# Three of an expert's four first matrices are prepared during the second products before it, in groups at the ends of row pairs; scratch results go to PSUM

## The chip, the cores and the metric

One core of a Trainium2 chip runs the whole program. The metric is the time of one execution in microseconds (us) of the device; the median of three runs of the kernel before is 1100.38 us, from 1098.74 to 1102.79. Engines are named as the profile names them: PE (TensorE, matrix products), PEld (its weight loads), DVE (VectorE), ACT (ScalarE), POOL (GpSimd), SP (the engine whose queue issues the transfers, "SPq" in the trace).

## The reference, cut to what matters

Three stages follow each other: attention with a learned bias, a first gated layer (MoE1), and a second layer with eight experts (MoE2). Only the third is touched.

```python
def _moe2_ref(x, w_gate, w1, w2):           # x 1152x512, w1 8x512x1024, w2 8x1024x512
    logits = x @ w_gate
    P = np.exp(logits - logits.max())
    for _ in range(8):
        P /= P.sum(1, keepdims=True) + 1e-09
        P /= P.sum(0, keepdims=True) + 1e-09
        P *= N / E
    out = np.zeros((N, D))
    for e in range(E):
        h = np.maximum(x @ w1[e], 0.0)
        out += P[:, e:e + 1] * (h @ w2[e])
    return out
```

## The kernel before, in words

Attention and MoE1 end at about 333 us; the rest is MoE2. Each float32 matrix is scaled by a power of two and split into a high and a low float16 part, and a product is made as high·high + high·low + low·high.

**First products.** `up(n)` makes a quarter of one expert's first product: n = 4e + q, expert e, quarter q. Each quarter consists of seven block products (a Strassen-like scheme that needs seven where eight would do), each of twelve matmuls (L1222), into PSUM banks `x`, `y`, `z`. Between them ACT copies banks out (`snap`, L1232), DVE joins them (`join`, L1236), and the result goes through a relu into float16 parts `hh` (ACT, L1240) and `hl` (DVE, L1245). The calls of `then(seg)` between the products, seg 0 to 6, take steps from the dictionary `extra`, which the main loop fills.

**Second products.** Expert 0 is done plainly, in two halves, `down_0(0)` after n = 2 and `down_0(1)` after n = 4: nine tiles of twelve matmuls each (`plain`, L1328) into a PSUM tile of tag "d", of which the pool `ps_d` has two; `add` (L1317 on ACT for the first half, L1319 on DVE otherwise) moves a tile to `acc`. The steps of the dictionary `todo` stand behind the tiles. For experts 1 to 7 `down(e)` takes eight of nine row tiles as four pairs i = 0 to 3, each with seven block products (L1404) and four main products (L1409) into banks px, py, pz. DVE first makes sums of blocks of the activations for the next pair (`sums`, L1397, eight instructions per pair) and adds each bank to `acc` (L1319). The ninth tile is plain, in two pieces, one ahead of the pairs and one behind them. The calls `more(i, k)`, k = 0 to 4, inside pair i take steps from `todo`.

**The work between.** All that prepares the next weights is written as steps that these dictionaries place:

- `prep(n, k)`: quarter n of w1. Step 0 scales it on ACT (L919) and issues the next load; 1 and 2 make sums of its blocks on DVE (L923 to L928, four instructions); 3 splits the plain blocks (ACT L931, POOL L932), 4 and 5 the sums (ACT L935, POOL L938).
- `p2(e, j)`: row block j of expert e's w2: ACT scales (L1016) and rounds it (L1017), POOL makes the low part `w2l` (L1018), and the next load is issued.
- `split_b(e)`: eight differences of w2 blocks on DVE (L1309).
- `pe(e, i)`: the largest absolute value of a quarter of w1 (i < 4, DVE, L754) or of a block of w2 (i ≥ 4, ACT, L102, which also writes a scratch result `junk`).
- `send(e, kind)`: DVE joins those maxima into `pj` (L788), SP writes them to DRAM (`peakse<-pj`) and reads all 128 back to every partition (`all<-peakse`). `power(e, kind)`: DVE reduces `all` (L751) and makes the power of two by which w1 (kind 1) or w2 (kind 2) is scaled.
- `gains(h)`: the factors for `add`.

The program order of each engine is the order of these calls; each engine and SP's queue run their own instructions in that order, and wait where an input or a buffer is not ready.

Of the kernel before, what the change touches and what calls it, by code (L numbers as in the profile page):

```python
# [9 lines left out]
F32 = mybir.dt.float32  # L10
# [3 lines left out]
F16 = mybir.dt.float16  # L14
# [9 lines left out]
DM = H * D  # L24
FF1 = 768
NE = 8
# [26 lines left out]
def make_body(stop=None):  # L53
    def body(tc, a):
        nc = tc.nc
        ctx = ExitStack()
        V, A, G, T = nc.vector, nc.scalar, nc.gpsimd, nc.tensor
# [18 lines left out]
        with ctx, tc.manual_schedule():  # L76
# [22 lines left out]
            mo, jk = [], []  # L99
# [641 lines left out]
            def peak_get(n):  # L741
                peak_send(n)
                if n in peaks_d:
                    src = peaks_d.pop(n)
                    w = src.shape[0]
                    peaks_s[n] = scl.tile([128, 256], F32, tag="all", name="all", bufs=2)[:, 0:w]
                    dma(peaks_s[n], src.unsqueeze(0).to_broadcast([128, w]))

            def peak_in(n, out):
# [68 lines left out]
            def peak_pow(m, items):  # L818

                if items:  # L820
                    for i, (h, kind) in enumerate(items):
                        o = scl.tile([128, 4], F32, tag=f"pw{kind}", name="pw", bufs=4)
# [6 lines left out]
            with ExitStack() as mctx:  # L829
# [79 lines left out]
                def prep_f(n):  # L909
# [4 lines left out]
                    hi = w1s.tile([128, 7, 2, 128], F16, tag="w1h", name="w1h")  # L914
                    lo = w1s.tile([128, 7, 2, 128], F16, tag="w1l", name="w1l")
                    w1s_t[n] = hi, lo

                    def scale():
# [82 lines left out]

                w2t, w2s = {}, []

                def prep_2(i):
# [78 lines left out]
            with ExitStack() as ectx:  # L1083
                h_p = ectx.enter_context(pool("h_p", bufs=2))
                w2s.append(ectx.enter_context(pool("w2t", bufs=2)))
                tp = ectx.enter_context(pool("tp"))
                jp.append(tp)
                sk = ectx.enter_context(pool("sk"))
                ps_d = ectx.enter_context(pool("ps_d", bufs=2, space=PSUM))
                banks = []  # L1090

                def use_banks(name):
# [243 lines left out]
                def run(fs):  # L1336
                    for f in fs:
                        f()
# [13 lines left out]
                def down_0(h):  # L1352
# [5 lines left out]
                                4: prep(3, 4, 5) + p2(0, 5), 5: p2(0, 6) + pe(1, 5), 6: p2(0, 7) + pe(1, 6),  # L1358
                                7: pe(1, 7), 8: power(1, 1) + prep(4, 0)}
                    else:  # L1360
                        todo = {0: prep(5, 0), 1: prep(5, 1), 2: prep(5, 2, 3), 3: power(1, 2) + p2(1, 0) + prep(5, 4, 5),
                                4: p2(1, 1, 2), 5: p2(1, 3), 6: p2(1, 4), 7: p2(1, 5), 8: p2(1, 6, 7)}
# [8 lines left out]
                w2_at = {1: [(2, 1), (2, 1), (2, 2), (2, 4), (3, 0), (3, 1), (3, 2), (3, 3)],  # L1371
                         2: [(1, 0), (1, 1), (1, 2), (1, 4), (2, 0), (2, 1), (2, 3), (2, 4)],
                         3: [(0, 0), (0, 2), (1, 0), (1, 2), (1, 4), (2, 1), (2, 3), (3, 0)]}

                def down(e):

# [35 lines left out]
                    todo = {}  # L1412
                    put = lambda i, k, fs: todo.setdefault((i, k), []).extend(fs)
                    if e < NE - 1:
                        put(0, 2, pe(e + 1, 3) + send(e + 1, 1))
                        put(2, 1, power(e + 1, 1) + prep(4 * e + 4, 0))
                        for i, k, ks in ((2, 2, (1,)), (2, 3, (2,)), (2, 4, (3, 4)), (3, 0, (5,))):
                            put(i, k, prep(4 * e + 4, *ks))
                        for i, k, ks in ((3, 1, (0,)), (3, 2, (1,)), (3, 3, (2, 3)), (3, 4, (4, 5))):
                            put(i, k, prep(4 * e + 5, *ks))  # L1420
                        if e < 3:
                            put(*((2, 0), (1, 0))[e - 1], power(e + 1, 2))
                        for j, at in enumerate(w2_at[min(e, 3)]):
                            put(*at, p2(e + 1, j))
                        if e > 1:
                            for j in range(4):
                                put(3, 1 + j, pe(e + 2, 4 + j))
                        put(3, 2, pe(e + 2, 0))
# [12 lines left out]
                    for i in range(4):  # L1441
# [24 lines left out]
                        prod(z2, A22, T4, False)  # L1466
                        prod(y, two(s[4]), B22, False)
                        run(nxt[4])
                        more(i, 2)
                        prod(x, two(s[3]), T3, False)  # L1470
# [20 lines left out]
                for n in range(4 * NE):  # L1491
                    e, q = divmod(n, 4)
                    extra = {}
                    put = lambda seg, fs: extra.setdefault(seg, []).extend(fs)
                    if n == 2:
                        put(1, prep(3, 0))
                    if n == 3:
# [9 lines left out]
                    if n == 1 or e and q in (1, 2):  # L1507
                        for seg, ks in ((0, (0,)), (1, (1, 2)), (2, (3,)), (3, (4, 5))):
                            put(seg, prep(n + 1, *ks))
                    if e and q == (1 if e == 1 else 0):  # L1510
                        b_s = split_b(e)
                    if e == 1:
                        for seg, k in {1: ((4, 0), (6, 1)), 2: ((5, 2), (6, 3), (6, 4)), 3: ((2, 5), (4, 6), (5, 7))}.get(q, ()):
                            put(seg, [b_s[k]])
                        if q in (1, 2):
                            put(5, pe(2, q - 1))
                        if q == 3:
                            for seg, i in ((0, 4), (1, 5), (2, 6), (4, 7)):
                                put(seg, pe(2, i))
                    elif e:  # L1520
                        for seg, k in {0: ((2, 0), (4, 1), (6, 2)), 1: ((6, 3),), 2: ((6, 4),), 3: ((2, 5), (4, 6), (5, 7))}[q]:
                            put(seg, [b_s[k]])
                        if q == 0:
                            put(5, pe(e + 1, 1))
                        if e == 2:
                            if q in (0, 3):
                                for j, seg in enumerate((0, 1, 2, 4)):
                                    put(seg, pe(3, 4 + j + 4 * (q > 0)))
                            if q == 3:
                                put(5, send(3, 2))  # L1530
                        elif q == 0:
                            for j, seg in enumerate((0, 1, 2, 4)):
                                put(seg, pe(e + 1, 8 + j))
                            put(6, send(e + 1, 2))
                        elif q == 3:
                            put(0, power(e + 1, 2))
                    if e and q == 3:
                        put(1, pe(e + 1, 2))
                    if e and q == (3 if e == 1 else 2):
                        put(3, [lambda: gains(e + 1)])  # L1540
                    up(n, extra)
                    if n in (2, 4):
                        down_0(n // 2 - 1)
# [63 lines left out]
```

## Time and profile before

| | |
|---|---|
| median of three runs | 1100.38 us (1098.74 to 1102.79) |
| the profiled execution, its own time | 1097.79 us |
| its span | 1096.0 us |
| PE busy | 1032.0 us, 94% |
| DVE busy | 862.4 us, 79% |
| ACT busy | 607.0 us, 55% |
| POOL busy | 326.9 us, 30% |

The span is what the trace covers of the profiled execution; its own time is 1.8 us longer. Busy shares are averages over stages that differ, so the stages are read one by one: a row of the windows view gives, for one stretch of the span, each engine's busy time and the clock granted to PE as a share of full speed. The view by time lists single instructions with their start and duration, and in brackets the idle time of the engine just before one and what ended it.

### The profile page before, as it was taken

The page shows a single profiled execution, that of the slowest core. Times are in us where ns is not written, and L with a number is a line of the kernel's source. Part 1 is how long each engine was busy: PE and PEld are TensorE (multiplying, and loading weights), DVE is VectorE, ACT ScalarE, POOL GpSimd, SP SyncE. Part 2 cuts the span into 40 slices and gives each one's busy share as a digit, 9 for nine tenths or more (in the row PEclk, how much of TensorE's full clock was granted, in tenths as well). Part 3 has the DMA queues.
Part 4 walks back from the last instruction along what each step waited for, and adds up shares of the span by engine and source line. Part 5 has one row for each costly group of instructions (what it writes and reads, how often), then busy time and mean ns, then how long its engine had stood idle before and what let it go on. Part 6 is the DMA issues. An engine that isn't in the chain of part 4 may idle for free. (4 is left out here: it accounts for less than half of the span.)

```text
span 1096.0 us, 21984 instructions
## 1 busy us (share of the span) xinstructions
PE 1032.0 (94%) x8842; PEld 805.8 (74%) x8842; DVE 862.4 (79%) x1706; ACT 607.0 (55%) x1116; POOL 326.9 (30%) x228
## 2 busy tenths in 40 slices
PE   8999999999999999898999998999899899989998
PEld 3267778999997565677777776877777687777787
DVE  8977775999588768887688789769778976976874
ACT  9989884444167675653662574366166436614710
POOL 6943532222141033302322422221242222124200
PEclk9999999999999999999999999999999999999999
DMA  6986652434210211202202210211121020100001
GB/s 190 286 271 193 204 151 95 139 113 102 94 62 23 59 61 53 85 2 54 88 20 54 69 41 11 80 30 42 51 68 42 11 81 29 42 3 1 1 20 68
DMA packets 39891, 84.58 MB, mean 77 GB/s; under 512 B 8100, under 2 KB 10732, under 8 KB 39788
## 3 DMA queue, kind: packets, MB, share of 16 engines
q1 hardware_dynamic: 39788, 83.17, 24.4%
q8 instruction: 69, 1.13, 0.5%
q14 instruction: 34, 0.28, 0.1%
HBM read 69.86 MB, written 13.30 MB: 76 GB/s over the span
## 5 line engine op out<-in xcount | busy, mean ns | idle before, releaser
L1222 PEld LDWEIGHTS <-w1h 128*128 128x128 f16 x1792 | 174.7, 98 | 73.7 <-issue 29.2
L1240 ACT ACTIVATE hh<-s 128x576 f16<-128x576 f32 x128 | 87.3, 683 | 122.3 <-DVE s L1236 84.7
L1018 POOL TENSOR_TENSOR w2l<-w2r,w2h 128x512 f16<-128x512 f32 x60 | 75.9, 1284 | 257.3 <-ACT w2h L1017 248.1
L932 POOL TENSOR_TENSOR w1l<-wf,w1h 128x768 f16<-128x768 f32 x32 | 56.5, 1764 | 279.6 <-ACT w1h L931 253.7
L1245 DVE SCALAR_TENSOR_TENSOR hl<-s,hh 128x576 f16<-128x576 f32 x128 | 107.0, 838 | 24.3 <-ACT hh L1240 21.2
L1404 PEld LDWEIGHTS <-s 128*128 128x128 f16 x896 | 89.7, 100 | 43.8 <-issue 31.1
L919 ACT ACTIVATE wf<-wr,pw 128x1024 f32<-128x1024 f32 x32 | 36.6, 1142 | 128.4 <-DVE pw L824 118.6
L1222 PEld LDWEIGHTS <-w1l 128*128 128x128 f16 x896 | 87.6, 98 | 22.1
L1409 PEld LDWEIGHTS <-hh 128*128 128x128 f16 x896 | 88.7, 99 | 16.0 <-issue 4.7
L1232 ACT ACTIVATE s<-x,cx 128x576 f32<-128x576 f32 x96 | 69.9, 728 | 20.9 <-PE x L1222 20.7
L1222 PE MATMUL x<-xth,w1h 128*128 128x288 f16 x384 | 78.4, 286 | 0.5 <-ACT s L1232 0.4
L1222 PE MATMUL x<-xth,w1l 128*128 128x288 f16 x384 | 78.4, 286 | 0.0
L1222 PE MATMUL x<-xtl,w1h 128*128 128x288 f16 x384 | 78.4, 286 | 0.0
L1404 PE MATMUL px<-t,s 128*128 128x256 f16 x448 | 60.8, 281 | 15.1 <-DVE acc L1319 14.8
L938 POOL TENSOR_TENSOR w1l<-wf,w1h 128x1024 f16<-128x1024 f32 x32 | 68.3, 2135 | 17.3 <-ACT w1h L935 17.3
L602 PE MATMUL m<-xh,wh 128*128 128x384 f32 x216 | 73.3, 339 | 0.0
L602 PE MATMUL m<-xh,wl 128*128 128x384 f32 x216 | 73.0, 338 | 0.0
L602 PE MATMUL m<-xl,wh 128*128 128x384 f32 x216 | 73.0, 338 | 0.0
L1319 DVE SCALAR_TENSOR_TENSOR acc<-px,kh,acc 128x256 f32<-128x256 f32 x112 | 53.1, 478 | 21.6 <-PE px L1404 15.9
L1222 PE MATMUL z<-xth,w1h 128*128 128x288 f16 x256 | 52.2, 286 | 17.0 <-DVE s L1236 17.0
L1236 DVE SCALAR_TENSOR_TENSOR s<-z,cx,s 128x576 f32<-128x576 f32 x64 | 52.0, 813 | 19.7 <-PE z L1222 16.3
L494 DVE CUSTOM_DVE_ANT_0 ng<-sc,bias 128x576 f32<-128x576 f32 x72 | 51.6, 754 | 15.5 <-PE sc L481 7.8
(259 smaller groups left out, 2802.1 us busy)
## 6 DMA issues: line engine op xcount, KB each, us to landing
wr<-in_moe_w SPq DMA_DIRECT2D x50, 512.0 KB, 3.5
w2r<-in_moe_w SPq DMA_DIRECT2D x64, 256.0 KB, 3.0
bias_f<-bo SPq DMA_DIRECT2D x36, 295.5 KB, 4.2
bias<-bias_f SPq DMA_DIRECT2D x32, 288.0 KB, 3.8
qk<-in_qk SPq DMA_DIRECT2D x6, 576.0 KB, 4.8
wr<-in_moe_w_out SPq DMA_DIRECT2D x6, 512.0 KB, 3.3
v<-in_v SPq DMA_DIRECT2D x4, 640.0 KB, 4.9
bias<-bias_f SPq DMA_DIRECT2D x16, 144.0 KB, 5.2
```

The lines of the kernel that those rows point to most:

```text
L602: T.matmul(out=p[:, :TG], lhsT=ws[:, 128 * c:128 * c + 128], rhs=xs[:, c, TG * g:TG * g + TG], start=(c == 0 and n == 0), stop=(c == 3 and ...
L932: G.tensor_tensor(out=lo[:, 0:3], in0=t[:, 1:4], in1=hi[:, 0:3], op=ALU.subtract)
L938: G.tensor_tensor(out=lo[:, 3:7], in0=t[:, 4:8], in1=hi[:, 3:7], op=ALU.subtract)
L1018: G.tensor_tensor(out=lo, in0=r, in1=hi, op=ALU.subtract)
L1222: T.matmul(out=ps[bank][:, s, :SH], lhsT=ws[:, i, c, :], rhs=xv[:, j, c, s * SH:s * SH + SH], start=(start and k == 0), stop=(k == 5), **kw)
L1232: A.activation(out=t, in_=src, func=AF.Identity, scale=c)
L1236: V.scalar_tensor_tensor(out=out, in0=z, scalar=scale, in1=out, op0=ALU.mult, op1=ALU.add)
L1240: A.activation(out=o, in_=src, func=AF.Relu)
L1245: V.scalar_tensor_tensor(out=l, in0=src, scalar=0.0, in1=o, op0=ALU.max, op1=ALU.subtract)
L1319: V.scalar_tensor_tensor(out=o, in0=ps, scalar=s, in1=o, op0=ALU.mult, op1=ALU.add)
L1404: T.matmul(out=out, lhsT=x[z][:, j], rhs=w[z][:, j], start=(start and j == z == 0), stop=(j == 3 and z == 1), skip_group_check=True)
L1409: T.matmul(out=out, lhsT=(ha, hb)[j // 4][0][:, j % 4, 128 * t:128 * t + 128], rhs=wh[:, j, n], start=False, stop=(j == 7), skip_group_che ...
```

## The change

What the kernel computes stays. Five things move:

1. `down(e)`, e = 1 to 6, prepares three quarters of the next expert's w1 (4e + 4 to 4e + 6), each scaled at step (i, 0) of pairs 1 to 3 and made at step (i, 3). Before it were two, spread over single steps of pairs 2 and 3. The eight `p2` of the next expert follow in groups of 4, 1, 1 and 2. The first group is preceded by `pace`, a tiny DVE copy of the scale from which ACT then reads. `power(e + 1, 1)` stands at (1, 0). For e = 1 `power(2, 2)` stands at (0, 4) instead of (2, 0).
2. `up` prepares one quarter of the next three instead of two. The maxima (`pe`), the sends and the steps of `split_b` stand at other segments.
3. `down_0(1)` also prepares quarter 6, and n = 5 to 6 quarter 7.
4. The scratch result `junk` of a sizing is a tile of `ps_d` (PSUM, tag "d") instead of one in SBUF.
5. Buffers: three instead of two for `w1h` and `w1l`, three instead of four for `pw`, and half the size for `all`.

For e = 1 `send(2, 2)` now stands in the last quarter of `up`, and the lines in `down` that size blocks 8 to 11 of expert 2 and send (2, 2) in pair 0 remain.

```diff
-                        junk = jp[0].tile([128, DM], F32, tag="jk", name="junk")
+                        junk = jp[0].tile([128, DM], F32, tag="d", name="junk")
...
-                jp.append(tp)
...
+                jp.append(ps_d)
...
+                def pace(e):
+                    if e < NE:
+                        paced[e] = scl.tile([128, 1], F32, tag="pc", name="pc", bufs=1)
+                        V.tensor_copy(out=paced[e], in_=w_pow[("e", e), 2][:, 2:3])
...
-                        s = w_pow[("e", e) if e else i // 4, 2][:, 2:3]
+                        s = paced[e] if e in paced else w_pow[("e", e) if e else i // 4, 2][:, 2:3]
...
-                                4: p2(1, 1, 2), 5: p2(1, 3), 6: p2(1, 4), 7: p2(1, 5), 8: p2(1, 6, 7)}
+                                4: p2(1, 1) + prep(6, 0), 5: prep(6, 1, 2) + p2(1, 2), 6: prep(6, 3, 4, 5) + p2(1, 3), 7: p2(1, 4, 5),
+                                8: p2(1, 6, 7)}
...
-                        put(0, 2, pe(e + 1, 3) + send(e + 1, 1))
-                        put(2, 1, power(e + 1, 1) + prep(4 * e + 4, 0))
...
+                        at = (0, 3)
+                        if e == 1:
+                            at = (0, 4)
+                            put(*at, power(2, 2))
+                        put(*at, [lambda: pace(e + 1)] + p2(e + 1, 0, 1, 2, 3))
+                        put(1, 0, power(e + 1, 1))
+                        for i in range(3):
+                            put(i + 1, 0, prep(4 * e + 4 + i, 0))
+                            put(i + 1, 3, prep(4 * e + 4 + i, 1, 2, 4, 5, 3) + p2(e + 1, *((4,), (5,), (6, 7))[i]))
+                        put(2, 1, pe(e + 2, 4, 5))
+                        put(2, 2, pe(e + 2, 6, 7))
+                        put(3, 1, pe(e + 2, 8))
...
+                        if q == 0 and e > 1:
+                            put(0, pe(e + 1, 9))
+                            put(2, t4(0, 1, 2))
+                            put(3, prep(n + 3, 0) + pe(e + 1, 10))
+                            put(4, pe(e + 1, 11))
+                            put(6, pe(e + 1, 0))
...
+                            if e == 1:
+                                put(0, pe(2, 10, 11))
+                                put(2, send(2, 2))
+                            else:
+                                put(0, power(e + 1, 2))
+                            put(1, pe(e + 1, 3))
+                            put(2, send(e + 1, 1) + (t4(4, 5, 6, 7) if e == 1 else t4(6, 7)) + [lambda: gains(e + 1)])
```

POOL's instructions in `down(4)`, before; `w2l` is a low part of the next expert's w2, `w1l` one of a w1 quarter (L932 the plain blocks, L938 the sums):

```order
L1018 TENSOR_TENSOR w2l<-w2r,w2h 128x512 x7
L932 TENSOR_TENSOR w1l<-wf,w1h 128x768
L938 TENSOR_TENSOR w1l<-wf,w1h 128x1024
L1018 TENSOR_TENSOR w2l<-w2r,w2h 128x512
L932 TENSOR_TENSOR w1l<-wf,w1h 128x768
L938 TENSOR_TENSOR w1l<-wf,w1h 128x1024
```

and after, where L1018 has become L1025:

```order
L1025 TENSOR_TENSOR w2l<-w2r,w2h 128x512 x4
L938 TENSOR_TENSOR w1l<-wf,w1h 128x1024
L932 TENSOR_TENSOR w1l<-wf,w1h 128x768
L1025 TENSOR_TENSOR w2l<-w2r,w2h 128x512
L938 TENSOR_TENSOR w1l<-wf,w1h 128x1024
L932 TENSOR_TENSOR w1l<-wf,w1h 128x768
L1025 TENSOR_TENSOR w2l<-w2r,w2h 128x512
L938 TENSOR_TENSOR w1l<-wf,w1h 128x1024
L932 TENSOR_TENSOR w1l<-wf,w1h 128x768
L1025 TENSOR_TENSOR w2l<-w2r,w2h 128x512 x2
```

Seven `w2l` in a row have become groups of 4, 1, 1 and 2, and a third quarter stands among them.

SP's queue from the end of expert 1's `up` into `down(1)`, before; `peakse` is a DRAM tile of maxima, `all` what is read back, `wr` and `w2r` are loads of w1 and w2:

```order
L60 DMA wr_6707<-in_moe_w 128x1024
L60 DMA peakse_7010<-pj 128x1
L60 DMA all<-peakse_7010 128x128
L60 DMA peakse_7052<-pj 128x1
L60 DMA all<-peakse_7052 128x128
L60 DMA wr_7265<-in_moe_w 128x1024
```

and after:

```order
L60 DMA wr_6587<-in_moe_w 128x1024
L60 DMA peakse_6879<-pj 128x1
L60 DMA all<-peakse_6879 128x128
L60 DMA peakse_6885<-pj 128x1
L60 DMA all<-peakse_6885 128x128
L60 DMA peakse_7031<-pj 128x1
L60 DMA all<-peakse_7031 128x128
L60 DMA w2r<-in_moe_w 128x512 x4
```

Two sends have become three, and loads of w2 follow them instead of one of w1.

ACT's instructions in `down_0(0)` behind the sixth tile stand in the same order before and after (here after, where L1317 has become L1324); the sizing's `junk` is now a tile of the pool that `d` is from:

```order
L1324 ACTIVATE acc<-d,kh 128x512
L102 ACTIVATE junk,pe<-w2r 128x512
L1324 ACTIVATE acc<-d,kh 128x512
L102 ACTIVATE junk,pe<-w2r 128x512
```

## Rows read from the trace of the kernel before

**Rows 1.** Windows of expert 1 to 7's pairs: window, length, busy by engine, clock, DMA.

```profile
479.82:526.30 46.48, 40.78 (x354) 35.12 (x353) 34.54 (x84) 22.15 (x38) 11.99 (x9) 0.96 0.22 55
...
575.93:621.66 45.73, 40.75 (x354) 35.13 (x352) 37.90 (x83) 17.25 (x28) 14.85 (x11) 0.96 0.29 73
671.76:716.09 44.33, 38.91 (x354) 34.42 (x353) 38.04 (x78) 16.57 (x28) 16.38 (x11) 1.00 0.24 73
765.96:811.94 45.98, 40.57 (x353) 35.28 (x352) 38.41 (x78) 16.55 (x28) 16.38 (x11) 0.96 0.22 71
861.81:907.66 45.85, 40.43 (x353) 35.14 (x352) 38.43 (x78) 16.57 (x28) 16.38 (x11) 0.96 0.22 71
957.53:1003.30 45.77, 40.36 (x353) 35.17 (x352) 37.97 (x79) 15.72 (x22) 16.11 (x11) 0.96 0.01 3
...
1050.91:1089.33 38.42, 38.42 (x353) 34.45 (x352) 25.58 (x64) 0.00 (x0) 0.00 (x0) 1.00 0.12 42
```

**Rows 2.** PE by time in `down(4)`: start, duration, instruction, idle before it.

```profile
774.47 0.37 PE L1404 MATMUL py<-w2l,s 128*128 128x256 f16 x1 [3.27 <-DVE acc L1319]
...
804.96 1.03 PE L1404 MATMUL px<-t,s 128*128 128x256 f16 x8 [1.59 <-DVE acc L1319]
```

**Rows 3.** DVE by time in `down(4)`, pair 0.

```profile
771.36 1.37 DVE L1397 TENSOR_TENSOR s<-hh 128x512 f16<-128x512 f16 x1
...
773.94 0.47 DVE L1319 SCALAR_TENSOR_TENSOR acc<-py,kh,acc 128x256 f32<-128x256 f32 x1
```

**Rows 4.** POOL by time, in `down(4)` and at the end of `down(6)`.

```profile
767.10 6.64 POOL L1018 TENSOR_TENSOR w2l<-w2r,w2h 128x512 f16<-128x512 f32 x5 [15.38 <-ACT w2h L1017]
...
995.48 2.13 POOL L938 TENSOR_TENSOR w1l<-wf,w1h 128x1024 f16<-128x1024 f32 x1 [1.91 <-ACT w1h L935]
997.56 1.16 POOL L1018 TENSOR_TENSOR w2l<-w2r,w2h 128x512 f16<-128x512 f32 x1
999.79 1.64 POOL L932 TENSOR_TENSOR w1l<-wf,w1h 128x768 f16<-128x768 f32 x1 [1.07 <-issue]
```

**Rows 5.** DVE by time in the last expert's `down(7)`, pair 1.

```profile
1064.61 0.42 DVE L1397 TENSOR_TENSOR s<-hh 128x512 f16<-128x512 f16 x1
...
1066.83 0.48 DVE L1319 SCALAR_TENSOR_TENSOR acc<-px,kh,acc 128x256 f32<-128x256 f32 x1
...
1067.56 0.42 DVE L1397 TENSOR_TENSOR s<-hl 128x512 f16<-128x512 f16 x1
```

**Rows 6.** PE by time in the same pair.

```profile
1069.25 1.04 PE L1409 MATMUL px<-w2h,hh 128*128 128x256 f16 x8
```

**Rows 7.** PE by time in expert 4's `up`: first and last of its gaps.

```profile
731.92 0.40 PE L1222 MATMUL z<-xth,w1h 128*128 128x288 f16 x2 [1.02 <-DVE s L1236]
...
758.96 0.41 PE L1222 MATMUL y<-xth,w1h 128*128 128x288 f16 x2 [0.40 <-ACT s L1232]
```

**Rows 8.** Groups of instructions: count, busy time, mean ns of one, idle before.

```profile
L102 ACT ACTIVATE junk<-w2r 128x512 f32<-128x512 f32 x60 | 37.1, 618 | 0.3
```

**Rows 9.** PE by time in n = 5.

```profile
454.90 0.40 PE L1222 MATMUL z<-xth,w1h 128*128 128x288 f16 x2 [2.30 <-DVE s L1236]
```

**Rows 10.** ACT by time in `down_0(0)`.

```profile
375.01 0.69 ACT L1317 ACTIVATE acc<-d,kh 128x512 f32<-128x512 f32 x1 [1.90 <-PE d L1328]
```

**Rows 11.** SP's queue by time in `down(1)`: start, time of the issue.

```profile
484.54 0.33 SPq L60 DMA_DIRECT2D peakse<-pj  x1
492.29 0.33 SPq L60 DMA_DIRECT2D all<-peakse  x1
492.74 0.35 SPq L60 DMA_DIRECT2D peakse<-pj  x1
502.14 0.32 SPq L60 DMA_DIRECT2D all<-peakse  x1
```

**Rows 12.** DVE by time in `down(1)`.

```profile
506.60 0.29 DVE L751 TENSOR_REDUCE pm<-all 128x1 f32<-128x128 f32 x1 [3.87 <-DMA all<-peakse]
```

**Rows 13.** PE by time at the same place.

```profile
507.90 1.56 PE L1404 MATMUL px<-t,s 128*128 128x256 f16 x8 [3.14 <-DVE acc L1319]
```

More of the change, by code (lines that the diff above doesn't have):

```diff
@@ L745, in peak_get @@
                     w = src.shape[0]
-                    peaks_s[n] = scl.tile([128, 256], F32, tag="all", name="all", bufs=2)[:, 0:w]
+                    peaks_s[n] = scl.tile([128, 128], F32, tag="all", name="all", bufs=2)[:, 0:w]
                     dma(peaks_s[n], src.unsqueeze(0).to_broadcast([128, w]))
@@ L821, in peak_pow @@
                     for i, (h, kind) in enumerate(items):
-                        o = scl.tile([128, 4], F32, tag=f"pw{kind}", name="pw", bufs=4)
+                        o = scl.tile([128, 4], F32, tag=f"pw{kind}", name="pw", bufs=3)
                         powers(o, m[:, i:i + 1])
@@ L913, in prep_f @@
                     t = w1s.tile([128, 8, 2, 128], F32, tag="wf", name="wf", bufs=1)
-                    hi = w1s.tile([128, 7, 2, 128], F16, tag="w1h", name="w1h")
-                    lo = w1s.tile([128, 7, 2, 128], F16, tag="w1l", name="w1l")
+                    hi = w1s.tile([128, 7, 2, 128], F16, tag="w1h", name="w1h", bufs=3)
+                    lo = w1s.tile([128, 7, 2, 128], F16, tag="w1l", name="w1l", bufs=3)
                     w1s_t[n] = hi, lo
@@ L1360, in down_0 @@
                     else:
-                        todo = {0: prep(5, 0), 1: prep(5, 1), 2: prep(5, 2, 3), 3: power(1, 2) + p2(1, 0) + prep(5, 4, 5),
-                                4: p2(1, 1, 2), 5: p2(1, 3), 6: p2(1, 4), 7: p2(1, 5), 8: p2(1, 6, 7)}
+                        todo = {0: prep(5, 0), 1: prep(5, 1), 2: prep(5, 2, 3), 3: power(1, 2) + prep(5, 4, 5) + p2(1, 0),
+                                4: p2(1, 1) + prep(6, 0), 5: prep(6, 1, 2) + p2(1, 2), 6: prep(6, 3, 4, 5) + p2(1, 3), 7: p2(1, 4, 5),
+                                8: p2(1, 6, 7)}
                     for t in range(NTT):
@@ L1414, in down @@
                     if e < NE - 1:
-                        put(0, 2, pe(e + 1, 3) + send(e + 1, 1))
-                        put(2, 1, power(e + 1, 1) + prep(4 * e + 4, 0))
[L1417 to L1428, printed above, removed]
+                        at = (0, 3)
[10 more added lines that the diff above has]
+                        put(3, 1, pe(e + 2, 8))
                     more = lambda *k: run(todo.get(k, ()))
@@ L1468, in down @@
                         run(nxt[4])
+                        prod(x, two(s[3]), T3, False)
                         more(i, 2)
-                        prod(x, two(s[3]), T3, False)
                         add(i + 4, n1, x, kh, h)
@@ L1494, in body @@
                     put = lambda seg, fs: extra.setdefault(seg, []).extend(fs)
+                    if n == 1:
+                        for seg, ks in ((0, (0,)), (1, (1, 2)), (2, (3,)), (3, (4, 5))):
+                            put(seg, prep(2, *ks))
                     if n == 2:
@@ L1506, in body @@
                         put(1, [lambda: cols(ps_d)])
-                    if n == 1 or e and q in (1, 2):
-                        for seg, ks in ((0, (0,)), (1, (1, 2)), (2, (3,)), (3, (4, 5))):
-                            put(seg, prep(n + 1, *ks))
+                        put(0, prep(7, 0))
+                        put(0, pe(2, 4))
                     if e and q == (1 if e == 1 else 0):
                         b_s = split_b(e)
[L1512 to L1516, printed above, removed]
-                        if q == 3:
[L1518 to L1540, printed above, removed]
+                    t4 = lambda *ks: [b_s[k] for k in ks]
+                    if e:
+                        if q == 0 and e > 1:
[4 more added lines that the diff above has]
+                            put(6, pe(e + 1, 0))
+                        if q == 1:
+                            put(0, prep(n + 2, 3) + (send(e + 1, 2) if e > 1 else []))
+                            put(2, prep(n + 2, 1, 2) + (t4(3) if e > 1 else []))
+                            put(6, pe(e + 1, 1))
+                            if e == 1:
+                                put(4, pe(2, 5))
+                                put(5, t4(0))
+                                put(6, t4(1))
+                        if q == 2:
+                            put(2, prep(n + 1, 4, 5) + pe(e + 1, 2))
+                            put(6, t4(2, 3) if e == 1 else t4(4, 5))
+                            if e == 1:
+                                for seg in (0, 1, 3, 4):
+                                    put(seg, pe(2, (6, 7, 0, 8, 9)[seg]))
+                                put(4, pe(2, 0))
+                        if q == 3:
+                            if e == 1:
+                                put(0, pe(2, 10, 11))
[4 more added lines that the diff above has]
+                            put(2, send(e + 1, 1) + (t4(4, 5, 6, 7) if e == 1 else t4(6, 7)) + [lambda: gains(e + 1)])
```

4 lines of the change are left out of this document (1 added, 3 removed).

## The prediction

> **What bounds the kernel now.** I read the windows by stage first. Experts 1 to 7 make their second products (`down`) from the same 352 matmuls. The last expert needs 38.42 us, and there PE is busy for the whole window at a granted clock of 1.00, the 2.4 GHz level throughout. Experts 2 to 6 take 45.73, 44.33, 45.98, 45.85 and 45.77, expert 1 takes 46.48, and in all of these but expert 3 the clock is 0.96, so a part of the window ran at 1.2 GHz [rows 1]. The window of the last expert differs in one thing: it has no next expert to prepare, its POOL column is 0.00 (14.85 to 16.38 in the five others), and DVE works 25.58 instead of about 38. So some 6 to 7.5 us of each middle `down` is not matmul work.
>
> In `down` of e=4 PE is idle for 45.98 − 40.57 = 5.41 us, and 40.57 − 38.42 = 2.15 more is matmuls that run slower [rows 1]. The timeline of PE shows where the idle time lies: gaps of 3.27 and 1.59 us, ended by the DVE's addition into `acc` [rows 2]. The timeline of DVE shows why the addition is late. The sums of activation blocks (L1397, both operands in SBUF) take 0.42 us when POOL is idle [rows 5] and 1.37 while POOL works, whereas the addition that reads PSUM takes 0.47 at the same place [rows 3]. POOL was making five `w2l` in a row there, 6.64 us [rows 4]. So the cost is not POOL's work but its meeting with the sums at the pair's middle.
>
> **The middle downs, e=2 to 6.** Now POOL's work of a `down` stands in four groups: four `w2l` at the third step of pair 0, held back by `pace`; then at the same step of pairs 1 to 3 one quarter each (L938, L932) and one or two `w2l`. The step stands behind the pair's last sums. Behind it DVE makes four additions of weights (0.42 each), ACT makes the high parts, then POOL runs 2.13 + 1.64 + 1.16 to 1.33 = 4.9 to 5.1 us [rows 4]. In the undisturbed expert a pair lasts 38.42 / 4 = 9.6 us and its sums, with the additions among them, go from 1064.61 to 1067.98 [rows 5]; the other 6.2 us hold no sum. The run starts some 2.5 us behind the step (1.7 of additions, then ACT), so it ends at about 7.6 and meets one sum or two, each longer by 0.95, about 1 to 1.9 us per pair. The addition that stands among the sums ends at 1067.31 [rows 5], and PE overwrites its bank at 1069.25 [rows 6]: 1.9 us to spare, so nearly all of it is hidden; I charge 0.5 per `down`. The four `w2l` of pair 0 come at ACT's pace and end at about 7 us, the same case. The four extra additions of weights per expert fall where DVE waits for PE. So 38.9 each instead of 227.66 for five: 227.66 − 194.5 = **−33.2**. If half of the loss stays it is −16.6.
>
> The Trainium skill ("SBUF — State Buffer", section "Who interferes with whom") says that a DVE instruction with two SBUF inputs and a GpSimd instruction that reads SBUF exclude each other, and that the later of the two waits for the whole of the other. The trace agrees as far as it goes: a sum takes 1.37 beside a `w2l` of 1.33. By the page a sum that meets the longer L938 would wait up to 2.13, which speaks against the change, since each group now begins with that instruction: two sums at 2.13 more would be 4.3 per pair, more than the 1.9 that I find to spare, and the middle downs would keep some half of their loss.
>
> **The first products, e=2 to 6.** In `up` of e=4 PE stands still four times, 2.58 us together, (the first and the last of the four in [rows 7]), mostly before a quarter's first `z` because DVE's join of the quarter before is late. Two of three preparations leave, with their DVE and POOL work. But the sizings move in: three of 0.62 [rows 8] and the scaling stand in one quarter on ACT, ahead of the copies that PE waits for, and the steps that split w2 stand in threes and pairs on DVE. By the ends: all but 0.6 of the gaps gone, −2.0; or 1.0 more, since each sizing or step that stands ahead of such a copy gives about its own 0.6. I take −0.7, near the middle, because the gaps only change place: 5 × −0.7 = **−3.5**; −0.5 for e=7.
>
> **n = 5 to 7 of e=1.** Gaps of up to 2.30 stand there [rows 9]. They lose preparations and gain the scaling of quarter 7 and eight sizings. Between −3 and +2; I take **−1**.
>
> **down_0(0).** The scratch output of the sizings is now a PSUM tile of the tag that the plain tiles use, with two buffers. A sizing behind tiles 2, 5, 6 and 7 takes the other buffer, so the next tile gets the buffer of the tile just made and PE waits for ACT's addition: it starts as the tile ends and takes 0.69 [rows 10]. With the hand-over about 1.0 each, four times: **+4** (2.8 to 6, the upper end with slower matmuls behind each). A sizing into PSUM may itself be a little shorter or longer than 0.62; ACT has room for either.
>
> **down_0(1)** gets the whole of `prep(6)`: 2.13 + 1.64 more on POOL [rows 4] and four additions on DVE, beside the row and column sums that PE's small matmuls wait for. Nothing if all of it is hidden, 3.8 if POOL's time is paid once: **+1.5**.
>
> **down(1).** Here the change adds a wait. The two maxima for expert 2 are now sent in the last quarter of `up`, and the w2 maximum is sent again in pair 0, where that line was not removed. A send is a write to DRAM and a read back on SP's queue, and SP holds the read until the write has landed: 484.54 to 492.29, and 492.74 to 502.14 [rows 11]; the data are there at 506.60 [rows 12]. So three such trips follow each other. The first starts about 8.5 us ahead of the pairs (6 of the quarter, 2.59 of the ninth tile's first piece). Three writes at 7.75 and two steps of 0.45 put the third read at 24.2 − 8.5 = 15.7 us, its data 4.5 later at 20.2; with 9.4 for one or two writes, up to 23.5. `power(2,2)`, which needs them, now stands at the end of pair 0, behind the last but one of its additions, 9.4 us into the pairs by the last expert's length of a pair (it was in pair 2). DVE waits 10.8 to 14 us. Behind it on DVE stand the additions that free PE's banks; PE has about 2 us of work before the first of them. Before, a wait of 3.87 gave a gap of 3.14 [rows 12, 13]. So 9 to 12 us of gap, 11 taken, 2 of slower matmuls as now, and 38.9: 51.9 against 46.48, **+5.5**. Bounds: −7.5 if the trips are over in time, +9.
>
> **Sum:** −33.2 − 3.5 − 0.5 − 1 + 4 + 1.5 + 5.5 = −27.2 on a profiled execution of 1097.79, 1070.6. The median of the runs is 2.6 higher, so about **1073**.
>
> **Rivals.** (A) POOL's groups are longer or later than their room: ACT's chain ahead of them is stretched, or they begin with the long instruction as a sum arrives. Against: 1.9 us to spare and a run that starts behind the sums. For: groups of 5 us in pairs of 9.6, whose sums want 3.4, leave 1.2. Half the loss stays, 16.6 more: 1090. (B) The repeated send doesn't hold DVE, because the first trips start earlier or are shorter than the rows show. For: the first two were made ahead on purpose. Against: SP's order, in which the third is the one that is waited for. 13 less: 1060. (C) Slower: the meeting merely moves, three groups per `down` where two stood, and each still costs PE 1.8 us (the 5.41 over three). Then the downs stay as they are, and the new stalls in down_0 and down(1) are what remains: −27.2 + 33.2 = +6, 1106. It decides once POOL's run overlaps four or more sums (4 × 0.95 is well over the 1.9 to spare); for it speaks that DVE has more to do in a `down` than before. (D) The groups aren't held: POOL runs on as soon as its inputs are there, through the sums of the same pair, and nothing changes: 1100. Against: each `w2l` needs ACT's output, and ACT stands behind the step.
>
> **How the numbers follow.** Forecast 0.55 (1064 to 1083 by the bounds of the up, down_0 and down(1) terms), A 0.20, B 0.12, C 0.08, D 0.05. From 1058 to 1092 all is held but C, D and the outer edges of A and B, about 0.2. About 0.5%, 5.5 us, is what a measurement of this kernel tells from no change: faster (under 1094.9) is the forecast, B and nearly all of A, 0.85; the same is D with parts of A and C, 0.08; slower 0.07.
>
> **What would show it.** Right: windows of `down` for e=2 to 6 near 39 with clock 1.00 and no gap over 1 us; sums of 0.42 in them but for one or two per pair; four gaps of about 1 us between plain tiles of down_0(0) ended by ACT's addition; in down(1) one wait of DVE on the read-back of over 10 us. Wrong: gaps of 2 us or more at the same place of pairs 1 to 3 (A or C); down(1) at 39 (B); an `up` above 46, if ACT's sizings weigh more than I take.

## The result and the profile after

The changed kernel takes 1069.6 us in the median (1068.96 to 1070.92), against 1099.6 for the kernel before (the three runs of the start and a fourth): a ratio of 0.9726, interval 0.970 to 0.975. The prediction was 1073, range 1058 to 1092. The span of the profiled execution falls from 1096.0 to 1069.1.

Windows of the changed kernel, columns as in [rows 1]: down(1), down(2), down(4), down(7), the `up` of expert 4, and down_0(0).

```profile
485.71:541.67 55.96, 41.48 (x352) 35.44 (x353) 35.43 (x89) 28.02 (x49) 14.57 (x10) 0.88 0.26 56
590.36:628.79 38.43, 38.43 (x354) 34.44 (x352) 31.00 (x82) 19.15 (x31) 14.59 (x11) 1.00 0.28 85
...
764.60:803.03 38.43, 38.43 (x354) 34.44 (x352) 31.02 (x82) 19.14 (x31) 14.59 (x11) 1.00 0.26 84
...
1024.17:1062.60 38.43, 38.43 (x353) 34.45 (x352) 25.42 (x64) 0.00 (x0) 0.00 (x0) 1.00 0.12 42
...
718.50:762.01 43.51, 42.22 (x337) 32.82 (x336) 33.77 (x55) 25.02 (x40) 7.10 (x5) 1.00 0.10 27
...
370.64:397.90 27.26, 24.48 (x117) 11.42 (x115) 18.81 (x48) 15.90 (x29) 8.27 (x6) 1.00 0.16 52
```

The middle downs of [rows 1] now take exactly what the last expert's takes, with PE busy throughout and the clock at 1.00 (2.4 GHz). POOL still works 14.59 us in each. Of the downs of experts 1 to 6 only down(1) has become longer, 55.96 for 46.48; down_0(0), of expert 0, has grown by 3.3 to 27.26.

In down(4), POOL's and then DVE's timeline around a group (before: [rows 3, 4]):

```profile
784.43 2.13 POOL L938 TENSOR_TENSOR w1l<-wf,w1h 128x1024 f16<-128x1024 f32 x1 [5.71 <-issue]
786.52 1.64 POOL L932 TENSOR_TENSOR w1l<-wf,w1h 128x768 f16<-128x768 f32 x1
788.12 1.34 POOL L1025 TENSOR_TENSOR w2l<-w2r,w2h 128x512 f16<-128x512 f32 x1
```

```profile
787.91 0.53 DVE L1401 TENSOR_TENSOR s<-hh 128x512 f16<-128x512 f16 x1
788.37 1.38 DVE L1401 TENSOR_TENSOR s<-hl 128x512 f16<-128x512 f16 x1
789.66 0.41 DVE L1401 TENSOR_TENSOR s<-s,hh 128x512 f16<-128x512 f16 x1
```

The group runs for 5.0 us and ends as the next pair's sums begin: one sum takes 1.38, one 0.53, the rest 0.41. PE has no gap there.

DVE's column for down(4) fell from 38.41 to 31.02, but that isn't less work. The same windows with the 32 sums alone, before, after, and for the last expert before, beside whom POOL is idle:

```profile
765.96:811.94 45.98, 17.40 (x32) 0.96 0.22 71
764.60:803.03 38.43, 12.70 (x32) 1.00 0.26 84
1050.91:1089.33 38.42, 11.41 (x32) 1.00 0.12 42
```

The sums were lengthened by 6.0 us before and are by 1.3 now. The additions of weights took 6.12 us for eight and now take 5.00 for twelve, so another 2.8 was lengthening. By this estimate DVE's own work in down(4) is 29.6 us before and 29.7 after: nearly the whole fall is the meeting with POOL that is gone.

In down_0(0), PE's gaps, two of four (the others 0.60 and 0.78):

```profile
379.35 0.38 PE L1335 MATMUL d<-w2h,hh 128*128 128x512 f16 x1 [0.60 <-ACT acc L1324]
...
388.26 0.38 PE L1335 MATMUL d<-w2h,hh 128*128 128x512 f16 x1 [0.80 <-ACT acc L1324]
```

In down(1), SP's queue, DVE and PE (before: [rows 11 to 13]):

```profile
478.75 0.33 SPq L60 DMA_DIRECT2D peakse<-pj  x1
486.46 0.33 SPq L60 DMA_DIRECT2D all<-peakse  x1
486.91 0.35 SPq L60 DMA_DIRECT2D peakse<-pj  x1
496.39 0.32 SPq L60 DMA_DIRECT2D all<-peakse  x1
497.10 0.32 SPq L60 DMA_DIRECT2D peakse<-pj  x1
506.57 0.32 SPq L60 DMA_DIRECT2D all<-peakse  x1
```

```profile
510.89 0.29 DVE L751 TENSOR_REDUCE pm<-all 128x1 f32<-128x128 f32 x1 [15.15 <-DMA all<-peakse]
```

```profile
512.76 1.86 PE L1408 MATMUL px<-t,s 128*128 128x256 f16 x8 [14.05 <-DVE acc L1326]
```

Three trips follow each other; DVE, at the end of pair 0, waits 15.15 us for the third, and PE 14.05.

### The profile page after: what moved, and what is told of

Same layout as the page of the kernel before. It is cut to its first block, busy times and chain, and to the rows that moved or that the text cites. A ratio compares the mean times of both kernels' runs of the same rounds, so it can differ in the third digit from the quotient of the medians.

```text
span 1069.1 us, 22013 instructions
## 1 busy us (share of the span) xinstructions
PE 1025.6 (96%) x8842; PEld 803.2 (75%) x8842; DVE 814.3 (76%) x1713; ACT 613.1 (57%) x1124; POOL 317.9 (30%) x228
## 4 chain that ended last, share of the span: by engine, by line
PE 61%; DVE 11%; ACT 8%; issue 3%; DMA 2%; DVEq 0%; SPq 0%; ACTq 0%
PE m L602 11%; PE px L1408 6%; PE x L1229 6%; PE d L1335 6%; PE y L1229 5%; PE z L1229 4%; PE pz L1413 4%; PE pz L1408 4%; PE py L1408 4%; PE o L1067 4%; DVE s L1243 3%; DVE hl L1252 3%; ACT hh L1247 2%; PE px L1413 2%; PE py L1413 2%
## 5 line engine op out<-in xcount | busy, mean ns | idle before, releaser
L1252 DVE SCALAR_TENSOR_TENSOR hl<-s,hh 128x576 f16<-128x576 f32 x128 | 99.4, 779 | 43.1 <-ACT hh L1247 40.4
L938 POOL TENSOR_TENSOR w1l<-wf,w1h 128x1024 f16<-128x1024 f32 x32 | 68.3, 2134 | 185.1 <-ACT w1h L935 100.0
L1025 POOL TENSOR_TENSOR w2l<-w2r,w2h 128x512 f16<-128x512 f32 x60 | 70.2, 1180 | 170.8 <-ACT w2h L1024 168.8
L1408 PEld LDWEIGHTS <-s 128*128 128x128 f16 x896 | 88.3, 99 | 26.2 <-issue 14.9
L932 POOL TENSOR_TENSOR w1l<-wf,w1h 128x768 f16<-128x768 f32 x32 | 53.8, 1681 | 177.5 <-ACT w1h L931 121.0
L1239 ACT ACTIVATE s<-x,cx 128x576 f32<-128x576 f32 x96 | 70.1, 730 | 13.3 <-PE x L1229 12.9
L935 ACT ACTIVATE w1h<-wf 128x1024 f16<-128x1024 f32 x32 | 33.7, 1054 | 60.7 <-DVE wf L928 60.7
L1023 ACT ACTIVATE w2r<-w2r,pc 128x512 f32<-128x512 f32 x48 | 34.0, 708 | 59.4 <-DVE pc L1009 59.4
```

The lines of the kernel that those rows point to most:

```text
L932: G.tensor_tensor(out=lo[:, 0:3], in0=t[:, 1:4], in1=hi[:, 0:3], op=ALU.subtract)
L938: G.tensor_tensor(out=lo[:, 3:7], in0=t[:, 4:8], in1=hi[:, 3:7], op=ALU.subtract)
L1239: A.activation(out=t, in_=src, func=AF.Identity, scale=c)
L1252: V.scalar_tensor_tensor(out=l, in0=src, scalar=0.0, in1=o, op0=ALU.max, op1=ALU.subtract)
L1408: T.matmul(out=out, lhsT=x[z][:, j], rhs=w[z][:, j], start=(start and j == z == 0), stop=(j == 3 and z == 1), skip_group_check=True)
```

## The experiments

Each compares with the changed kernel at 1069.6 us unless it says otherwise.

**one_send: the second send removed, and the four sizings that it repeats.**

```diff
-                    if e == 1:
-                        run(pe(2, 8, 9, 10, 11))
...
-                        if e == 1 and i == 0:
-                            run(send(2, 2))
```

> Theory: in down(1) DVE waits 15.15 us because the w2 maximum of expert 2 is sent a second time and SP's queue makes three trips one after the other (writes issued at 478.75, 486.91 and 497.10 in the changed kernel). Without the second send two trips are left. The w2 maximum is then back about 5 us into the pairs, ahead of power(2,2); the w1 maximum is back at about 501.1, and power(2,1) stands in pair 1 at about 496.6, so a DVE wait of 4 to 5 us and a PE gap of 1 to 3 remain. down(1) falls from 55.96 to 41 to 43 us, the whole to 1054 to 1058 us. Rival: the place of the two powers, early in the pairs, is the cause, and any send would be late: a wait of 10 us or more stays, the whole 1065 to 1070 us.

1054.5 us (1054.4 to 1054.7), 15.1 less; against the kernel before 0.9587 (0.955 to 0.962). The window of down(1), then DVE's only wait on a read-back there, and the longest gap of PE:

```profile
484.51:525.54 41.03, 39.51 (x352) 34.30 (x353) 34.40 (x88) 25.22 (x41) 14.54 (x10) 1.00 0.29 76
```

```profile
498.72 0.29 DVE L751 TENSOR_REDUCE pm<-all 128x1 f32<-128x128 f32 x1 [2.37 <-DMA all<-peakse]
```

```profile
500.04 0.27 PE L1408 MATMUL py<-w2l,s 128*128 128x256 f16 x1 [0.78 <-DVE acc L1326]
```

The power's early place is not the trouble: with two trips the wait is 2.37 and the gap 0.78. The longest gap is 13.3 us shorter and the matmuls take 39.51 for 41.48, which covers the 14.9 of the window and leaves nothing for the four sizings on ACT. The third trip is what cost 15 us, so the repeated send, left in the code, takes a third of the gain that the change would have.

**no_pace: the first group not held.**

```diff
-                        put(*at, [lambda: pace(e + 1)] + p2(e + 1, 0, 1, 2, 3))
+                        put(*at, p2(e + 1, 0, 1, 2, 3))
```

> ACT reads the scale directly, without the small DVE copy that holds the first group of four w2 blocks; DVE's work is one copy less per expert. Theory (the meeting of POOL's instructions with DVE's sums is the cost): the group runs about 1 us after a down begins, beside the eight sums of pair 0, sums of 1.37 us come back there, PE has a gap of 2 to 3.5 us before py of pair 0 and slower matmuls behind it: 3 to 5 us more in each down of experts 2 to 6, the whole 1085 to 1095 us. Rival (the middle downs are free because DVE has less to do in them, whenever POOL works): downs stay at 38.4, the whole 1068 to 1071 us.

1090.9 us (1089.9 to 1092.9), 21.3 more. In down(4) (769.81 to 813.03, 43.22 us) POOL, two of DVE's sums, and PE:

```profile
771.01 5.35 POOL L1025 TENSOR_TENSOR w2l<-w2r,w2h 128x512 f16<-128x512 f32 x4 [16.50 <-ACT w2h L1024]
```

```profile
771.38 1.39 DVE L1401 TENSOR_TENSOR s<-s,hl 128x512 f16<-128x512 f16 x1
...
775.28 1.37 DVE L1401 TENSOR_TENSOR s<-hh 128x512 f16<-128x512 f16 x1
```

```profile
777.43 0.37 PE L1408 MATMUL py<-w2l,s 128*128 128x256 f16 x1 [2.31 <-DVE acc L1326]
```

As the theory had it. The program places the four blocks behind pair 0's sums all the same. In the changed kernel ACT waits 7.82 us for the copy `pc`, and POOL's group starts 9.1 us into the down:

```profile
772.27 0.72 ACT L1023 ACTIVATE w2r<-w2r,pc 128x512 f32<-128x512 f32 x1 [7.82 <-DVE pc L1009]
```

Without the copy ACT runs ahead of DVE, POOL follows it, and the group starts 1.2 us into the down. So place in the program alone doesn't keep two engines apart: the small copy, which ties ACT to DVE's progress, is worth 21 us here.

**pool_twice: POOL's groups longer, nothing else.**

```diff
-                        G.tensor_tensor(out=lo[:, 0:3], in0=t[:, 1:4], in1=hi[:, 0:3], op=ALU.subtract)
+                        for _ in range(2 if n > 7 and n % 4 < 3 else 1):
+                            G.tensor_tensor(out=lo[:, 0:3], in0=t[:, 1:4], in1=hi[:, 0:3], op=ALU.subtract)
...
-                        G.tensor_tensor(out=lo[:, 3:7], in0=t[:, 4:8], in1=hi[:, 3:7], op=ALU.subtract)
+                        for _ in range(2 if n > 7 and n % 4 < 3 else 1):
+                            G.tensor_tensor(out=lo[:, 3:7], in0=t[:, 4:8], in1=hi[:, 3:7], op=ALU.subtract)
```

> POOL makes the two low parts of each w1 quarter in down twice, with the same result, so a group is 8.8 instead of 5.0 us; nothing is added on DVE, ACT or PE. Theory: the groups of pairs 1 and 2 now reach over four to six of the next pair's sums, each 0.95 or more longer, DVE is 4 to 6 us late against 1.9 to spare, and PE gets a gap of 2 to 4 us per pair and slower matmuls: 4 to 9 us per down in six downs, the whole 1095 to 1125 us. The Trainium skill (SBUF — State Buffer, section Who interferes with whom) has the later of the two instructions wait for the whole of the other: then sums beside L938 (2.13 us) or L932 (1.64 us) take longer than the 1.37 seen beside w2l. Rival (POOL is off the path, and its length in a down doesn't matter): 1068 to 1073 us.

1129.3 us (1128.8 to 1131.0), 59.7 more and a little above what I expected, and slower than the kernel before (1.027, 1.024 to 1.030). Windows of a down and of an `up`, then POOL, two of four lengthened sums, and PE in that down:

```profile
793.14:835.66 42.52, 40.26 (x354) 35.26 (x353) 31.90 (x76) 17.35 (x28) 22.30 (x14) 0.96 0.18 58
741.98:790.55 48.57, 43.21 (x337) 33.46 (x337) 36.59 (x55) 27.64 (x44) 14.42 (x8) 0.96 0.08 25
```

```profile
817.21 3.61 POOL L933 TENSOR_TENSOR w1l<-wf,w1h 128x768 f16<-128x768 f32 x2
```

```profile
819.24 1.86 DVE L1403 TENSOR_TENSOR s<-s,hh 128x512 f16<-128x512 f16 x1
821.02 1.37 DVE L1403 TENSOR_TENSOR s<-s,hl 128x512 f16<-128x512 f16 x1
```

```profile
823.51 1.03 PE L1415 MATMUL px<-w2h,hh 128*128 128x256 f16 x8 [2.27 <-DVE acc L1328]
```

Four sums in a row meet POOL (1.08, 1.86, 1.86 and 1.37 us), and PE's gap is 2.27: the rival C of the prediction, with four sums as its point, is what happens here. But a gap of this size comes once per down, not twice, and a down gets only 3 to 4 us longer, and the ninth tile's piece behind it 0.6 to 1.6. The larger part, 5 to 6.5 per expert and some 34 of the 60, is in `up`, by a way that I had not expected. ACT and PE there:

```profile
753.87 0.60 ACT L102 ACTIVATE junk<-w2r 128x512 f32<-128x512 f32 x1 [3.04 <-DMA w2r<-in_moe_w]
```

```profile
756.95 0.64 PE L1231 MATMUL x<-xth,w1h 128*128 128x288 f16 x2 [4.53 <-ACT s L1241]
```

POOL's late `w2l` frees its buffer late, the load into that buffer is issued 9.3 us into the `up` (2.2 in the changed kernel), and the sizing that waits for the load stands on ACT ahead of a copy that PE waits for.

**junk_y: the four scratch results of down_0(0) in bank y.**

```diff
-                        junk = jp[0].tile([128, DM], F32, tag="d", name="junk")
+                        if e == 1 and i < 8:
+                            junk = banks[0].tile([128, 512], F32, tag="y", name="junk")
+                        else:
+                            junk = jp[0].tile([128, DM], F32, tag="d", name="junk")
```

> The four scratch results of down_0(0) go to the bank y of the first products, which is idle there, instead of to a buffer of the plain tiles; all else as changed. Theory (the scratch result takes the second buffer of tag d, so the next tile waits for ACT's addition): the four gaps of 0.60 to 0.80 us are gone, down_0(0) falls from 27.26 to about 24 us, the whole 1066 to 1067 us. Rival (ACT is held by writing to PSUM beside PE, or the tiles wait for ACT's other work): the gaps stay, 1069 to 1070 us.

1064.1 us (1063.9 to 1065.9), 5.5 less, more than either theory gives. The window of down_0(0):

```profile
370.01:393.96 23.95, 23.95 (x116) 11.27 (x114) 18.84 (x48) 15.88 (x29) 8.34 (x6) 1.00 0.19 57
```

27.26 has become 23.95, with no gap: the buffer was the cause, 3.3 us. The rest lies elsewhere: the profiled executions differ by 4.9 us, of which 1.0 is in down(1), where the third trip's wait gave a gap of 13.0 and not 14.05, and 0.6 is ahead of the third stage. The run `both` below has the same edit without a third trip, and gains 3.2 by it.

**dve_more: six reductions on DVE in each down.**

```diff
+                        def idle_max(q):
+                            m = scl.tile([128, 1], F32, tag="pm", name="jr", bufs=2)
+                            peak(m, w1r[q].rearrange("p b c f -> p (b c f)"))
+
+                        for i in range(3):
+                            for k in (3, 4):
+                                put(i, k, [lambda q=4 * e + 7: idle_max(q)])
```

> Six more reductions of a w1 quarter (1.21 us each, one SBUF input, result unused) on DVE in each down of experts 1 to 6, at steps 3 and 4 of pairs 0 to 2: DVE's work in a down goes back from 31 to about 38 us, what it was before the change; POOL's groups stay where they are. Theory (the meeting of POOL with the sums was the cost, not DVE's load): downs of experts 2 to 6 stay at 38.4 to 39.5, since a reduction stands where DVE waits for PE, the whole 1069 to 1076 us. Rival (the change works because DVE has 7 us less to do in a down): downs back at 44 to 46, the whole 1100 to 1110 us.

1080.7 us (1080.4 to 1081.2), 11.1 more: between the two. A down, one of the reductions, the first sum behind it, and PE:

```profile
769.28:809.70 40.42, 38.75 (x354) 34.37 (x353) 36.16 (x88) 19.15 (x31) 14.41 (x11) 1.00 0.24 80
```

```profile
787.79 1.21 DVE L754 TENSOR_REDUCE jr<-wr 128x1 f32<-128x1024 f32 x1
...
793.62 0.62 DVE L1401 TENSOR_TENSOR s<-hh 128x512 f16<-128x512 f16 x1
```

```profile
792.14 1.03 PE L1408 MATMUL px<-t,s 128*128 128x256 f16 x8 [0.87 <-DVE acc L1326]
```

The sums are not slower than after the change: the 32 take 11.83 us. But the expectation read the 38 us of before as work. By the estimate above 8.8 of them were lengthening, so this run doesn't give the old load back; it puts DVE's own work 6 us above that of either kernel. Even so the down takes 40.42 and not 45.98: the added load costs 2.0 per down, where two reductions stand close together ahead of an addition, and the theory's bound of 39.5 was too low.

**w2_alone: the kernel before with the w2 blocks moved alone.**

```diff
-                         2: [(1, 0), (1, 1), (1, 2), (1, 4), (2, 0), (2, 1), (2, 3), (2, 4)],
-                         3: [(0, 0), (0, 2), (1, 0), (1, 2), (1, 4), (2, 1), (2, 3), (3, 0)]}
+                         2: [(1, 3), (1, 3), (1, 3), (1, 3), (2, 3), (2, 3), (3, 3), (3, 3)],
+                         3: [(0, 3), (0, 3), (0, 3), (0, 3), (1, 3), (2, 3), (3, 3), (3, 3)]}
...
+                        if e > 1:
+                            put(*w2_at[min(e, 3)][0], [lambda: pace(e + 1)])
```

> The kernel before, with one part of the change alone: for experts 3 to 6 the first w2 blocks wait behind the small copy at step 3 of pair 0 (of pair 1 in expert 2), the w1 quarters stay where they were in pairs 2 and 3. Since only the first block is held, six low parts run in a row behind it. Theory: the gaps of 3.27 and 0.55 in pair 0 of downs 3 to 6 go, at most a gap of 1 to 2 comes in pair 1, where the row of 7 us reaches two or three sums; the gap of 1.6 in pair 3 stays, since the w1 quarters still meet its sums. Downs of 40 to 43 instead of 44.3 to 46, the whole 1080 to 1090 us; about half of the change's gain in the downs is the w2 blocks. Rival (the w1 quarters at the pair ends are what counts): 1096 to 1101 us.

1068.5 us (1066.5 to 1069.0), 0.9714 of the kernel before: as fast as the whole change, where I had expected 1080 to 1090. Down(4), and PE's one gap in it:

```profile
754.36:793.66 39.30, 38.67 (x354) 34.43 (x352) 34.47 (x79) 16.08 (x25) 13.56 (x10) 1.00 0.21 69
```

```profile
786.67 1.03 PE L1410 MATMUL px<-t,s 128*128 128x256 f16 x8 [0.63 <-DVE acc L1325]
```

(`pace` and its use are added as in the change.) Downs 3 to 6 take 39.30 and down(2) 40.57. So 6.7 of 7.55 us in down(4) come from the w2 blocks and their copy. The gap of pair 3 has shrunk from 1.59 to 0.63 too, and the slower sums of pair 1 (0.68, 1.38, 1.37) cost nothing. The 32 sums still take 15.55 us here, 4.1 above the undisturbed 11.41, so most of the lengthened sums of this down cost PE nothing: what counts is which sums they are. No run moves the w1 quarters alone. The `up` of the middle experts stays at 44.7. The whole change does better than this in every middle expert, and loses it again in down_0(0) and down(1), which this version leaves nearly as they were.

**both: one_send and junk_y together.**

> The changed kernel without the second send and its sizings, and with the four scratch results of down_0(0) in the idle bank y. Theory (the two costs are independent, one after the other on PE): 1069.6 - 15.1 - 3.3 to 5.5 = 1049 to 1051.5 us. Rival (the one hides a part of the other): 1052 to 1055 us.

1051.3 us (1050.9 to 1051.9), 0.9557 (0.954 to 0.957): the two costs add up, 18.3 below the changed kernel, which is 15.1 and the 3.3 of the buffer less 0.1. It beats both kernels.

**tuned: steps moved at two places in that.**

```diff
-                                8: p2(1, 6, 7)}
+                                8: p2(1, 6, 7) + prep(7, 0) + pe(2, 4)}
...
-                        put(0, prep(7, 0))
-                        put(0, pe(2, 4))
...
-                                put(0, power(e + 1, 2))
+                                put(3, power(e + 1, 2))
```

> As the run both, and two steps moved: the scaling of quarter 7 and one sizing from n = 5 to the last tile of down_0(1), and power(e + 1, 2) from segment 0 to segment 3 of the last quarter of up, for experts 2 to 6. Theory (in n = 5 these 1.9 us on ACT stand ahead of a copy that PE waits for; in the last quarter the power's 0.95 us on DVE stand ahead of the join that ACT and then PE's y wait for): the gap of 1.63 in n = 5 goes, and of the y gaps of 1.12 about 0.8 each go: 5 to 6 us less than both, 1044 to 1046 us. Rival (the gaps come from the steps of split_b at the quarter's end before): at most 2 us less than both.

1051.1 us (1050.7 to 1051.4), where I had expected 1044 to 1046: no difference that can be told. (The gaps in question are 0.84 and 1.34; the expectation's 1.12 and 1.63 hold a matmul of 0.28 as well.) Expert 4's `up` and down(4), first of both, then of tuned:

```profile
699.02:742.53 43.51, 42.22 (x338) 32.83 (x336) 33.77 (x55) 25.02 (x40) 7.09 (x5) 1.00 0.09 27
745.12:783.55 38.43, 38.43 (x354) 34.45 (x353) 31.02 (x82) 19.14 (x31) 14.60 (x11) 1.00 0.26 84
```

```profile
699.05:741.77 42.72, 42.22 (x337) 32.83 (x336) 33.13 (x54) 24.39 (x39) 7.09 (x5) 1.00 0.09 27
744.37:783.38 39.01, 38.84 (x353) 34.35 (x353) 32.01 (x83) 19.76 (x32) 14.58 (x11) 1.00 0.27 82
```

The first sum on DVE, of both and of tuned:

```profile
745.68 0.42 DVE L1404 TENSOR_TENSOR s<-hh 128x512 f16<-128x512 f16 x1
```

```profile
745.71 0.42 DVE L1404 TENSOR_TENSOR s<-hh 128x512 f16<-128x512 f16 x1
```

The `up` is 0.79 shorter, as expected, and the down 0.58 longer. At the end of `up` DVE has a chain of its own, which ends at the same moment in both; PE now arrives earlier and waits for the sums. The join was the releaser of the gap, but DVE's whole load in that stretch was its bound: in both runs DVE works without a pause from 731.7 to 741.1, and the power stands in that row either way. In n = 5 the gap before y fell from 1.34 to 0.57, but one of 0.88 came before x, and n = 5 to 7 take 0.6 longer.

## Why the prediction was right, and where its sum was off

| term | predicted | measured |
|---|---|---|
| downs of experts 2 to 6 | −33.2 | −35.5 |
| ups of experts 2 to 6 | −3.5 | −5.3 |
| up of expert 7 | −0.5 | −1.0 |
| n = 5 to 7 | −1 | +0.6 |
| down_0(0) | +4 | +3.3 |
| down_0(1) | +1.5 | +0.6 |
| down(1) | +5.5 | +9.5 |

These make −27.8, and the span fell by 26.9. Against the gain stand the ninth tile's first piece of expert 1 (0.5 longer) and the third stage's start (1.1 later, ahead of all that the change touches in it); smaller parts give 0.7 back.

**The middle downs** held in mechanism and size. The run of 5.0 us and one sum or two beside it are what the trace after shows, and they cost nothing instead of 0.5. That the meeting, not DVE's load, was the cause is shown from four sides: DVE's own work is the same before and after by the estimate above, no_pace brings 4.8 of 7.55 us back by bringing the meeting back with one tiny copy less on DVE, pool_twice makes the downs 3 to 4 us longer with the same DVE instructions, and dve_more adds 7.2 us to DVE's work without the meeting and costs 2.0. So the prediction's comparison of DVE's 25.58 with about 38 took lengthening for work, and so did the argument for C that DVE has more to do than before. What is not shown is how the last 0.9 us per down (39.30 in w2_alone to 38.43) divide between the w1 quarters' place and that of the reductions and sizings that left the downs. **Rival A** weighed the long instruction ahead of a sum. It didn't come about because the long one stands first in its group and is over before the next sums.

**down(1)** was mis-sized, and lies just outside my bound of +9. The step that failed is the length of the chain. I took the shorter of the two writes in [rows 11] (7.75) for all three, and a start 8.5 us ahead of the pairs. The first write took 7.7, but the second and the third held SP for 9.5 each, and the start was 7.0 ahead (478.75 to 485.71): the data came at 510.9, 25.2 us into the pairs, where I had 20.2 to 23.5. So DVE waited 15.15 where I had 10.8 to 14, and PE's gap was 14.05 where I had 9 to 12. **Rival B**, that the chain is over in time, needed the third trip to be gone: one_send shows 1054.5 for it, below the 1060 that I gave.

**down_0(0)** is the predicted wait, four gaps of 0.60 to 0.80; the term of 1.0 each counted a little too much for the hand-over, for which no run has a figure.

**down_0(1)** paid once, with a gap of 1.18 that DVE's addition ends. Ahead of that addition stand two additions of weights of `prep(6)`, 1.27 and 1.86 us long beside POOL: the same meeting, added here.

**The ups** gained more than I took. The meeting was in them too: in each `up` of experts 2 to 6 before, two `hl` stood beside an L938 and took about 1.7 and 1.2 us instead of 0.76, ahead of two of the three late joins. This is one of them in expert 4's:

```profile
739.65 1.69 DVE L1245 SCALAR_TENSOR_TENSOR hl<-s,hh 128x576 f16<-128x576 f32 x1 [0.75 <-ACT hh L1240]
```

After the change no `hl` in these stages takes more than 0.8. The gaps before z are gone; the largest that is left is one before y in the last quarter, ended by ACT:

```profile
757.61 0.41 PE L1229 MATMUL y<-xth,w1h 128*128 128x288 f16 x2 [0.84 <-ACT s L1239]
```

**n = 5 to 7** lost instead of gaining, within its bounds of −3 to +2. Before, two gaps of 2.30 and 2.08 ended by DVE's join made most of the idle time; now it is several smaller ones, the longest of 1.34 and 1.35 ended by ACT's copies. That the sizings and the scaling on ACT are their cause isn't shown: `tuned`, which takes two of these steps out of n = 5, didn't shorten it.

The total was closer than its parts, and that is luck: the downs and ups brought 4.6 us more than predicted, and down(1) took 4.0 more. So the profiled execution took 1070.9, where the sum had 1070.6.

## What to carry to other kernels

Where two engines slow each other, first ask when they meet, not how much they work: moving POOL's instructions by a few microseconds gave 5 to 6.7 us per down in w2_alone, and the order in the program didn't do it without a dependence that ties the free engine to the busy one. An engine that is held up still counts as busy: compare the time of the same instructions in a disturbed and an undisturbed stage before calling a busy column work. When a step is moved earlier, look for the old line that still does it: a repeated round trip through DRAM, serial on its queue, cost more here than any stage gained. A gap's releaser is not yet its bound: move a step off the releaser's path only after reading whether its engine has room in the whole stretch.

## What the hardware showed that was not expected

A DVE sum beside a POOL instruction is lengthened by what is left of that instruction, and then takes its turn: 1.37 to 1.39 us beside `w2l`, and 1.86 beside the L933 of pool_twice, whose two took 3.61. The Trainium skill ("SBUF — State Buffer", section "Who interferes with whom") says that the later of the two waits for the whole of the other, and these runs agree. The full length shows in pool_twice, in down(1), where a sum starts 0.06 us behind the long instruction (there L940) and takes 2.35:

```profile
523.59 2.35 DVE L1403 TENSOR_TENSOR s<-hh 128x512 f16<-128x512 f16 x1
```

The POOL instruction is lengthened too, a `w2l` from 1.15 to 1.33.

In the chain of down(1) a round trip of the maxima right behind another was slower: the first write held SP's queue 7.7 us in the changed kernel, the two behind it 9.5 each. In the kernel before it was 7.75 and 9.4 [rows 11], in one_send 6.9 and 9.4. Why isn't shown; one trip with none just before it, at 733.3 in the changed kernel, took 9.2 as well.

The sizing's instruction took 0.618 us on average with its scratch result in SBUF and 0.593 with it in PSUM, as the group of [rows 8] and the same group of the changed kernel show:

```profile
L102 ACT ACTIVATE junk<-w2r 128x512 f32<-128x512 f32 x64 | 38.0, 593 | 0.6
```
